# Attention beside a gated MLP on one core: query norm rows summed in one bank, key offset from a weight, gate by pairs

## Chip, core and metric

The kernel runs on one core of one Trainium2 chip. The metric is the device time in microseconds of one execution. The engines are called by their names in the profile: PE (TensorE), ACT (ScalarE), DVE (VectorE), POOL (GpSimd) and SP (the queue that issues most DMAs).

## What is computed

x is 2048 tokens by 448 features. Cut to what matters:

```python
xn = layernorm(x)
q, k, v = split(xn @ wqkv)            # 16 heads of 28
s = softmax(q @ k.T * 28**-0.5) @ v   # per head, 2048 x 2048 scores
s = s @ wo
g = silu(gelu_tanh(xn @ w1 + b1) @ w2 + b2)   # 448 -> 1792 -> 448
out = x + s * g
```

All inputs and the output are bfloat16.

## The kernel before

**Tiles.** The heads form four groups (g) of four, the queries four chunks (c) of 512. A block is a pair (g, c), 16 in all, run in the order b = 4g + c. Inside a block there are 16 key tiles of 128 for each of four heads: 64 units of 128 keys x 512 queries, 1024 units in the kernel (the last block is cut along the queries so that its end can be finished in pieces). A unit is a score matmul into a PSUM bank (`t_score`, L1158), an exp that turns it into a bfloat16 tile P, and a PV matmul (`pv_task`, L1417) that adds to the accumulator bank `acc`. Head features are padded from 28 to 32, so four heads fill the 128 partitions: score matmuls are row tiles, PV matmuls column tiles of the PE array.

**Two places for exp.** Most units get their exp on ACT (`p_exps`, L1217), which reads two or three banks of the PSUM ring in one instruction. The others, called late units, are done on DVE (`p_late`, `p_exp2`): the score goes into a side bank (ring bank 3 or the bank `misc`), L1262 moves it scaled to SBUF, and three scalar_tensor_tensor instructions (L1347, L1348, L1350) on one or two units at a time turn it into a bfloat16 exp by a polynomial. The result lies in one of five plates until PV has used it.

**Offset of the exp.** Each query and key carries a 29th feature. On the key side it is -1, on the query side a norm term: half the sum of squares of the query plus a constant from the norms of the key weights (`colK`). Thus a score has an upper bound taken off, and no maximum over keys is needed. The key's -1 is added at eviction (`t_kev`, L727, with the column `ecol[:, 2:3]`). The query's term is made tile by tile in `p_q`: eviction (L946), square (L951), a matmul with the selector `bsel` that sums the squares of each head into row 28 of its 32 (L953, in a second bank), and L956, which adds that bank, the constant and the query. The first chunk of group 0 has a path of its own (`p_q0`).

**The other branch.** The first layer (`p_f1`, L1011) is projected between attention blocks and kept in SBUF. At unit GM = 582 ACT switches its table and does all gelus in one stage (`p_gelu`, L1066), half from SBUF and half from PSUM (`p_direct`, which takes the ring; bank 3 is then not free for others). The second layer (`p_f2`, L1087 with eviction L1092) follows as soon as a chunk's gelu is done, so its first tile runs inside the gelu stage; then tanh on ACT and the gate on DVE tile by tile (`p_silu`, L1102 and L1105), and at the end `p_out`/`p_last`.

**What sets the order.** Each engine's instructions are written in a fixed order that is found while the program is built. Every piece of work is a generator that yields tasks with an engine, estimated durations, the buffers read and written, and a priority; `run` repeatedly takes the task that could start first, and among those within 0.1 us the best priority. Free PSUM banks go to the generators in the order of their numbers (`settle`). How many units become late is decided by `pick(k)`: DVE's backlog must not exceed `THS` of the block (in us), and the work must fit into what is left of the block plus `SLACKS` of the block:

```python
left = (n - 1 - r) * 0.452 + SLACKS[m // 64]
...
return (k == 1 or bl <= THS[m // 64]) and bl + k * (LC + 0.69) <= left
```

**Buffers of P.** `NP` buffers of 512 columns take the results of ACT's exps. From the time when the staged weights are no longer needed until 24 units before the gelu stage, free parts of the buffer h serve as 21 more, and after it parts of xnT as 15 more (`p_room`). An exp waits until the PV of its buffer's former unit has run.

**Queues.** Loads and stores go over SP in program order, and a DMA that waits there for an engine holds those behind it. The load of w2 is such a one; it is issued when the later scratch of DVE (in kT) has replaced the one inside w2's buffer.

Of the kernel before, what the change touches and what calls it, by code (L numbers as in the profile page):

```python
# [8 lines left out]
ALU = mybir.AluOpType  # L9
# [15 lines left out]
NRING = 6  # L25
NP = 21
NBLK = G * C
# [3 lines left out]
LC = 1.85  # L31
THS = (1.0, 6.0, 6.0, 6.0, 6.0, 5.0, 5.0, 5.0, 6.0, 6.0, 6.0, 6.0, 9.0, 6.0, 6.0, 6.0)
SLACKS = (9.0, 9.0, 9.0, 9.0, 8.5, 9.0, 7.0, 6.5, 6.5, 9.0, 9.5, 9.0, 8.5, 9.0, 9.0, 9.0)
SM_SCALE = DH ** -0.5
# [39 lines left out]
class _Kernel:  # L74
# [21 lines left out]
    def sb(self, name, shape, dtype=dt.bfloat16):  # L96
        return self.es.enter_context(self.nc.sbuf_tensor(name, shape, dtype))
# [160 lines left out]
    def alloc(self):  # L258
# [17 lines left out]
        self.E_sb = sb("E_sb", [128, 2, 512], bf)  # L276
        self.qsq = sb("qsq", [128, 2, 512], bf)
        self.ident = sb("ident", [128, 128], bf)
        self.bsel = sb("bsel", [128, 128], bf)
        self.sel = sb("sel", [128, 4], bf)  # L280
        self.iota_p = sb("iota_p", [128, 1], f32)
        self.ecol = sb("ecol", [128, 4], f32)
# [70 lines left out]
        self.b_wz, self.b_h2s = B(), B()  # L353
        self.b_qsq = [B(), B()]
        self.b_rc, self.b_rhl, self.b_colK, self.b_csq = B(), B(), B(), B()
# [19 lines left out]
        self.s_x2 = [self.sem("s_x2%d" % q) for q in range(4)]  # L375
        self.s_b1 = self.sem("s_b1")
        self.s_x0b, self.s_wqk1 = self.sem("s_x0b"), self.sem("s_wqk1")
        self.s_out = [self.sem("s_out%d" % q) for q in range(10)]
        self.s_w = {n: self.sem("s_" + n) for n in ("wqk", "wv", "w1", "w2", "wo", "b")}

    def schedule(self):
# [9 lines left out]
        K.stg_done = 0  # L391
        K.qsqs = [0, 1]
        K.f2n = [0] * C
        K.pv_started = False
# [58 lines left out]
        for c in (1, 2, 3):  # L453
            K.spawn(K.p_q(1, c), nxt())
        f1 = deque(SBT)
        for c in range(C):
            for _ in range(4):
                K.spawn(K.p_f1(*f1.popleft()), nxt())
            K.spawn(K.p_k(2, c), nxt())
            K.spawn(K.p_q(2, c), nxt())  # L460
        while f1:
            K.spawn(K.p_f1(*f1.popleft()), nxt())
        for c in range(C):
            K.spawn(K.p_k(3, c), nxt())
            K.spawn(K.p_q(3, c), nxt())
        K.spawn(K.p_gelu(), 0)
        K.spawn(K.p_direct(), 0)
# [14 lines left out]
    def constants(self):  # L482
# [3 lines left out]
        def f(eng):  # L486
# [12 lines left out]
            return eng.memset(K.xn[:, :, :, D:D + 1], 1.0)  # L499
        e(DVE, f, writes=[K.b_pads], dur=1.6)  # L500

        def late_pads():
# [49 lines left out]
        def f(eng):  # L552
# [3 lines left out]
        e(POOL, lambda eng: eng.tensor_copy(selb, K.sel[:, :, None].to_broadcast([128, 4, 32])), reads=[K.b_bsel],  # L556
          writes=[K.b_selb], dur=0.3)
        K.b_hf[1][0].r.append(K.b_bsel.w)

# [161 lines left out]
    def t_kev(self, E, g, c, bank, tok, prio=2):  # L721
        K = self
        dst = K.kT[:, g, c * 512:(c + 1) * 512]
        if E == ACT:
            fn = lambda eng: eng.activation(dst, bank, ACTF.Identity, bias=K.ecol[:, 2:3])
        else:
            fn = lambda eng: eng.tensor_scalar(dst, bank, K.ecol[:, 2:3], None, op0=ALU.add)  # L727
        return _Task(E, fn, [tok, K.b_cols], [K.b_kT[g][c]], 0.75, 0.0, prio)

# [20 lines left out]
    def p_first(self):  # L750
# [66 lines left out]
        def kproj(h):  # L817
            bank, tok = ring(4 * h + 1)
            for k in range(2):
                yield proj(1, h, k, bank, tok)  # L820
            yield _Task(ACT, lambda eng: eng.activation(K.kT[:, 0, 256 * h:256 * h + 256], bank[:, 0:256], ACTF.Identity,
                                                        bias=K.ecol[:, 2:3]),
                        [tok, K.b_cols] + ([K.b_kT0] if h else []), [K.b_kT[0][0] if h else K.b_kT0], 0.45, 0.0, 1 + h)
# [65 lines left out]
    def p_norm(self, g0, g1, pr=1):  # L889
        K = self  # L890
        bank, tok = yield ("bank",)
        n = g1 - g0

        def f(eng):
            ins = None
            for g in range(g0, g1):
                for kt in range(KT):
                    ins = eng.matmul(bank[:, g:g + 1], K.wsq[:, kt, 128 * g:128 * (g + 1)], K.ones[:, :],
                                     start=(kt == 0), stop=(kt == KT - 1), skip_group_check=True)
            return ins  # L900
        yield _Task(PE, f, K.b_wsq[g0:g1] + [K.b_pads], [tok], 0.15 * n + 0.1, 0.1, pr, 0.15)
        for b in K.b_hf[1]:
            b.r += [x.w for x in K.b_wsq[g0:g1]] + K.b_wsq[g0].r
        yield _Task(DVE, lambda eng: eng.tensor_copy(K.csq[:, g0:g1], bank[:, g0:g1]), [tok], [K.b_csq], 0.17, 0.0, pr)

        def f(eng):
            return eng.matmul(bank[:, 8 + g0:8 + g1], K.bsel[:, :], K.csq[:, g0:g1], start=True, stop=True)
        yield _Task(PE, f, [K.b_csq, K.b_bsel], [tok], 0.05, 0.15, pr)
        yield _Task(DVE, lambda eng: eng.tensor_scalar(K.colK[:, g0:g1], bank[:, 8 + g0:8 + g1], KNORM, K.coff[:, 0:1],
                                                       op0=ALU.mult, op1=ALU.add), [tok, K.b_cols], [K.b_colK], 0.17, 0.0, pr)  # L910
        K.banks.append((bank, tok))
# [27 lines left out]
    def p_q(self, g, c):  # L939
        K = self  # L940
        bank, tok = yield ("bank", lambda: K.ready(K.b_xnT[c] + [K.b_wqk[0][g], K.b_colK, K.b_kT[0][3]]) and ((g, c) == (0, 1) or K.boot()))
        for k in range(2):
# [4 lines left out]
        K.banks.append((bank, tok))  # L947
        yield ("until", lambda: len(K.qsqs) > 0)
        i = K.qsqs.pop(0)
        qs, tq = K.qsq[:, i, :], K.b_qsq[i]  # L950
        yield _Task(DVE, lambda eng: eng.tensor_tensor(qs, qb, qb, ALU.mult), [qr], [tq], 0.43, 0.0, 2)  # L951
        bank2, tok2 = yield ("bank", lambda: K.ready([tq]) and (g == 0 or K.norms_done))
        yield _Task(PE, lambda eng: eng.matmul(bank2, K.bsel[:, :], qs, start=True, stop=True),  # L953
# [3 lines left out]
                                                              op1=ALU.add), [tok2, K.b_colK, qr], [qr, K.b_qT[g][c]], 0.75, 0.0, 2)  # L957
        K.banks.append((bank2, tok2))

    def t_v(self, ts, h0, h1, bank, tok):  # L960
# [117 lines left out]
    def p_f2(self, c, t):  # L1078
        K = self
        bank, tok = yield ("bank", lambda: K.b_h[c].tw is not None and K.ready([K.b_h[c], K.b_w2]) and (c < 2 or K.g_done[c - 2]))  # L1080
        hv = K.h[:, c, :].rearrange("p (f n) -> p f n", n=512)
# [15 lines left out]
    def p_silu(self, c):  # L1097
# [5 lines left out]
                    [K.b_fsb[c % 2]], [K.b_sig[c % 2]], 0.1 + 0.375 * nt, 0.0, 0)  # L1103
        for t in range(nt):
            yield _Task(DVE, lambda eng, t=t: eng.scalar_tensor_tensor(K.g_sb[:, c, t, :], sg[:, t, :], 1.0, fb[:, t, :],  # L1105
                                                                       op0=ALU.add, op1=ALU.mult),
                        [K.b_sig[c % 2], K.b_fsb[c % 2]], [K.b_h[c], K.b_g[c]], 0.63, 0.0, 3)
        K.g_done[c] = True
# [498 lines left out]
```

The softmax here doesn't subtract the row's maximum and nothing guards it: scores larger than these inputs give would overflow.

## Time and profile before

The time is 472.9 us (median of three runs, 472.8 to 472.96); the profiled execution spans 471.2 us.

| engine | busy, us | share of span |
|---|---|---|
| ACT | 459.1 | 97% |
| PE | 439.9 | 93% |
| DVE | 408.6 | 87% |
| POOL | 42.5 | 9% |

| group (line, engine) | count | mean ns of one |
|---|---|---|
| L1217 ACT exp of two units | 202 | 1108 (into P) |
| L1217 ACT exp of three units | 171 | 1551 (into P) |
| L1066 ACT gelu, gelu stage from 256 to 283 us | 14 | up to 2345 |
| L1347, L1348, L1350 DVE exp by polynomial, two units | 153 | 1223 (L1347) |
| L951 DVE square of the query | 15 | 423 |
| L1105 DVE gate | 15 | 620 |
| L878 PE matmuls on a zero weight that keep PE busy | 684 | 220 |

The means of instructions that overlap their neighbours include the overlap, so count times mean is more than the busy time. PE's share contains L878, work that changes no result (a zero weight), and so is no measure of how full PE is. A line in the costliest groups gives busy time, mean duration of one, and the idle time of the engine just before, with what ended it.

### The profile page before, as it was taken

To read this page: it belongs to the slowest core of one execution; us is meant where nothing else is said; L and a number is where in the kernel's file an instruction comes from. 1 tells how busy PE (TensorE), PEld (TensorE's weight loads), DVE (VectorE), ACT (ScalarE), POOL (GpSimd) and SP (SyncE) were. 2 spreads that over 40 slices of the span, in tenths; PEclk is the share of its full clock that TensorE was granted. 3 is DMA by queue.
4 is the path that set the end of the run, shared out by engine and by line. 5 is a ranking of instruction groups with operands and counts; after the bars stand their busy time and mean duration, and the time that the engine had idled before them with its cause. 6 is when DMAs were issued, how large, how long until landed. Compare 5 with 4: busy or idle time off the path is not lost.

```text
span 471.2 us, 10607 instructions
## 1 busy us (share of the span) xinstructions
PE 439.9 (93%) x4407; PEld 175.2 (37%) x4440; DVE 408.6 (87%) x581; ACT 459.1 (97%) x417; POOL 42.5 (9%) x78
## 2 busy tenths in 40 slices
PE   6999999999999999999999999999999989999995
PEld 5442333333323233323333343333333443433552
DVE  8946999899899998998898959768898988989986
ACT  6999999999999999999999999999999999999994
POOL 7480100001000101001010100010010000010001
PEclk9999999999999999999999999999999999999999
DMA  8401000000000000000220000000110010101001
GB/s 265 141 2 36 2 1 0 1 2 2 1 0 1 1 1 2 2 0 1 70 69 2 1 0 1 11 30 1 41 39 1 1 40 3 40 1 40 3 22 60
DMA packets 8289, 11.11 MB, mean 24 GB/s; under 512 B 1649, under 2 KB 6897, under 8 KB 8242
## 3 DMA queue, kind: packets, MB, share of 16 engines
q1 hardware_dynamic: 7954, 9.75, 6.7%
q8 instruction: 35, 0.57, 0.5%
q10 hardware_dynamic: 288, 0.69, 0.4%
q14 instruction: 12, 0.10, 0.1%
HBM read 8.61 MB, written 1.84 MB: 22 GB/s over the span
## 4 chain that ended last, share of the span: by engine, by line
PE 46%; ACT 39%; issue 13%; DVE 1%; ACTq 0%; DVEq 0%
ACT P L1217 23%; PE ring L1158 12%; ACT h L1217 9%; PE acc L1417 7%; ACT xnT L1217 6%; PE ring L1028 5%; PE acc L878 4%; PE ring L1087 4%; PE misc L1087 3%; PE misc L716 2%; PE ring L716 2%; PE ring L970 1%; PE misc L1028 1%; PE acc L860 1%; PE misc L970 1%
## 5 line engine op out<-in xcount | busy, mean ns | idle before, releaser
L1217 ACT ACTIVATE P<-ring 128x1024 bf16<-128x1024 f32 x210 | 237.8, 1305 | 0.6 <-PE ring L1158 0.6
L1158 PE MATMUL ring<-qT,kT 32*128 32x512 bf16 (+2 forms) x1086 | 144.8, 359 | 16.6 <-ACT P L1217 6.4
L1217 ACT ACTIVATE h<-ring 128x1536 bf16<-128x1536 f32 (+1 forms) x97 | 111.3, 1292 | 1.0 <-PE acc L1417 0.7
L1158 PEld LDWEIGHTS ring<-qT,kT 32*128 32x128 bf16 x1086 | 37.5, 91 | 139.0 <-ACT P L1217 68.9
L1217 ACT ACTIVATE xnT<-ring 128x1536 bf16<-128x1536 f32 x66 | 77.6, 1350 | 0.0
L878 PE MATMUL acc<-ident,zero 128*128 128x128 bf16 x684 | 55.5, 220 | 0.5 <-issue 0.5
L1262 DVE TENSOR_SCALAR x_sb<-misc 128x512 f32<-128x512 f32 x64 | 44.0, 688 | 8.8 <-PE misc L1158 7.8
L1417 PE MATMUL acc<-P,vaug 128*32 128x512 bf16 (+2 forms) x587 | 50.0, 357 | 0.3 <-DVE x_sb L1350 0.3
L1489 POOL CAST rhi<-rc 128x16 bf16<-128x16 f32 x15 | 12.4, 824 | 395.2 <-DVE rc L1487 291.8
L878 PEld LDWEIGHTS acc<-ident,zero 128*128 128x128 bf16 x684 | 39.2, 98 | 21.5 <-issue 19.1
L1262 DVE TENSOR_SCALAR x_sb<-ring 128x512 f32<-128x512 f32 x43 | 29.6, 688 | 12.6 <-PE ring L1158 12.5
L1347 DVE SCALAR_TENSOR_TENSOR kT<-x_sb 128x1024 f32<-128x1024 uint16 (+1 forms) x32 | 38.1, 1189 | 1.8
L1348 DVE SCALAR_TENSOR_TENSOR kT<-kT 128x1024 f32<-128x1024 f32 (+1 forms) x32 | 37.8, 1183 | 0.4
L1028 PE MATMUL ring<-xnT,w 128*128 128x512 bf16 x141 | 36.6, 381 | 0.9 <-issue 0.8
L1087 PE MATMUL ring<-w,h 128*128 128x448 bf16 x140 | 33.9, 355 | 0.0
L1347 DVE SCALAR_TENSOR_TENSOR w<-x_sb 128x1024 f32<-128x1024 uint16 (+1 forms) x24 | 27.6, 1149 | 0.1
L1348 DVE SCALAR_TENSOR_TENSOR w<-w 128x1024 f32<-128x1024 f32 (+1 forms) x24 | 27.6, 1150 | 0.1
L1158 PE MATMUL misc<-qT,kT 32*128 32x512 bf16 (+1 forms) x66 | 24.6, 377 | 0.2 <-DVE w L1092 0.2
L1417 PE MATMUL acc<-h,vaug 128*32 128x512 bf16 x239 | 24.0, 384 | 0.0
L1350 DVE SCALAR_TENSOR_TENSOR x_sb<-kT,x_sb 128x1024 uint16<-128x1024 f32 x19 | 23.2, 1219 | 0.2
L1028 PE MATMUL misc<-xnT,w 128*128 128x512 bf16 x68 | 19.2, 381 | 1.1 <-issue 0.8
L1087 PE MATMUL misc<-w,h 128*128 128x448 bf16 x84 | 20.0, 355 | 0.0
(179 smaller groups left out, 550.9 us busy)
## 6 DMA issues: line engine op xcount, KB each, us to landing
h<-in_A_x_dram SPq DMA_DIRECT2D x4, 448.0 KB, 3.3
w<-in_B_w_dram SPq DMA_DIRECT2D x1, 1568.0 KB, 7.4
w<-in_B_w_dram SPq DMA_DIRECT2D x1, 1344.0 KB, 8.1
out_dram<-h SPq DMA_DIRECT2D x6, 224.0 KB, 2.0
x_sb<-in_A_x_dram SPq DMA_DIRECT2D x2, 448.0 KB, 5.8
h<-in_A_wqkv_dram SPq DMA_DIRECT2D x3, 168.0 KB, 5.3
x_sb<-in_A_x_dram ACTq DMA_DIRECT2D x1, 448.0 KB, 5.1
out_dram<-h SPq DMA_DIRECT2D x4, 112.0 KB, 1.7
```

The source lines that it names most:

```text
L716: ins = eng.matmul(bank, w[:, kt, g * 128:(g + 1) * 128], K.xnT[:, kt, c * 512:(c + 1) * 512], start=(kt == 0), stop=(kt == KT - 1))
L878: ins = eng.matmul(K.acc[:, 0:128], K.zero[:, :], K.ident[:, :], start=False, stop=True, skip_group_check=True)
L1028: ins = eng.matmul(bank, K.w1[:, kt, ft * 128:(ft + 1) * 128], K.xnT[:, kt, c * 512:(c + 1) * 512], start=(kt == 0), stop=(kt == KT - 1))
L1087: ins = eng.matmul(ps, hv[:, ft, t * 128:(t + 1) * 128], K.w2[:, ft, :], start=(ft == 0), stop=(ft == FT - 1))
L1158: return eng.matmul(dst, K.kT[32 * j:32 * j + 32, g, t * 128:(t + 1) * 128], K.qT[32 * j:32 * j + 32, g, c * 512 + q0:c * 512 + q0 + nq], ...
L1217: return eng.activation(reg[:, i0:i0 + n, :], K.ring[:, b0:b0 + n, :], ACTF.Exp, scale=SM_SCALE)
L1262: yield _Task(DVE, lambda eng, i=i, half=half, bank=bank: eng.tensor_scalar(K.ysb[i][:, 512 * half:512 * half + 512], bank, SM_SCALE * LOG ...
L1347: yield _Task(DVE, lambda eng: eng.scalar_tensor_tensor(u, lo, EXP_A, lo, op0=ALU.add, op1=ALU.mult), ty, [tu], d, 0.0, 4)
L1348: yield _Task(DVE, lambda eng: eng.scalar_tensor_tensor(u, u, EXP_B, u, op0=ALU.add, op1=ALU.mult), [tu], [tu], d, 0.0, 4)
L1350: yield _Task(DVE, lambda eng: eng.scalar_tensor_tensor(pl.bitcast(dt.uint16), u, EXP_K, y, op0=ALU.mult, op1=ALU.add), ty + [tu], [K.b_pl ...
L1417: return eng.matmul(K.acc[32 * j:32 * j + 32, q0:q0 + nq], K.vaug[:, t, 4 * g + j, :], ap[:, col:col + nq], tile_position=(0, 32 * j), sta ...
L1489: yield _Task(POOL, lambda eng: eng.tensor_copy(K.rhi[:, :], K.rc[:, :]), [K.b_rc], [K.b_rhl], 1.1, 0.0, 1)
```

## The change

It has five parts, and new values of the planner's thresholds.

- Query norm, groups 1 to 3: a tile is only evicted and squared. When all four chunks of a group are squared (four buffers `qsq`), four column-tiled matmuls with a narrow selector `bsel4` put the sums of all of them into one bank, one chunk per 32 partitions. One tensor_scalar adds the constants (`colK2`) and writes `qst`, and four DMAs on SP copy four rows each into the rows 28, 60, 92 and 124 of qT. Group 0 keeps the old path.
- Key offset: a -1 is written once into the weight wk, at the row that meets the feature of xn that is always 1. Key evictions are then plain copies.
- Gate: two tiles in one instruction.
- Side bank in gelu: `p_f2` doesn't start before all gelus from PSUM have been placed, so that `misc` serves late units until then.
- The new buffers take the room of three P buffers: NP goes from 21 to 18.

```diff
-NP = 21
+NP = 18
...
-THS = (1.0, 6.0, 6.0, 6.0, 6.0, 5.0, 5.0, 5.0, 6.0, 6.0, 6.0, 6.0, 9.0, 6.0, 6.0, 6.0)
-SLACKS = (9.0, 9.0, 9.0, 9.0, 8.5, 9.0, 7.0, 6.5, 6.5, 9.0, 9.5, 9.0, 8.5, 9.0, 9.0, 9.0)
+THS = (1.0, 5.0, 11.0, 6.0, 6.0, 5.0, 6.0, 5.0, 6.0, 6.0, 6.0, 6.0, 6.0, 6.0, 5.0, 11.0)
+SLACKS = (6.0, 7.0, 8.0, 10.0, 8.0, 6.0, 7.5, 8.5, 9.0, 7.5, 5.5, 8.0, 10.0, 10.0, 7.5, 4.5)
...
-        self.qsq = sb("qsq", [128, 2, 512], bf)
+        self.qsq = sb("qsq", [128, 4, 512], bf)
+        self.qst = sb("qst", [128, 512], bf)
...
+        e(DVE, lambda eng: eng.memset(K.wk[64:65, 3, :].rearrange("p (h e) -> p h e", e=32)[:, :, DH:DH + 1], -1.0),
+          writes=[K.b_pads], dur=0.1)
...
+        bs4 = K.bsel[:, :].rearrange("p (j e) -> p e j", e=32)[:, 24:32, :]
+        e(POOL, lambda eng: eng.tensor_copy(K.bsel4[:, :].rearrange("p (e j) -> p e j", j=4), bs4), reads=[K.b_bsel],
+          writes=[K.b_bsel4], dur=0.2)
...
-            fn = lambda eng: eng.tensor_scalar(dst, bank, K.ecol[:, 2:3], None, op0=ALU.add)
+            fn = lambda eng: eng.tensor_copy(dst, bank)
...
+    def p_qn(self, g):
+        K = self
+        bank, tok = yield ("bank", lambda: len(K.qn[g]) == C and K.ready(K.b_qsq) and K.norms_done)
+
+        def f(eng):
+            ins = None
+            for c in range(C):
+                ins = eng.matmul(bank[32 * c:32 * c + 32, :], K.bsel4[:, :], K.qsq[:, c, :], tile_position=(0, 32 * c),
+                                 start=True, stop=True, skip_group_check=True)
+            return ins
+        yield _Task(PE, f, K.b_qsq + [K.b_bsel4], [tok], 0.226, 0.17, 4, mode="col")
+        K.qn_done = g
+        yield _Task(DVE, lambda eng: eng.tensor_scalar(K.qst[:, :], bank, K.colK2[:, g:g + 1], None, op0=ALU.add),
+                    [tok, K.b_colK2], [K.b_qst], 0.75, 0.0, 2)
+        K.banks.append((bank, tok))
+        for c in range(C):
+            dst = bass.AP(tensor=K.qT, offset=28 * G * S + g * S + 512 * c, ap=[[32 * G * S, 4], [1, 512]])
+            K.dma(SP, lambda eng, c=c, dst=dst: eng.dma_start(dst, K.qst[32 * c + 16:32 * c + 20, :]), K.s_qn[g][c],
+                  reads=[K.b_qst, K.qn[g][c]], writes=[K.b_qT[g][c]], land=max(K.now, K.b_qst.tw) + 2.5)
...
-        bank, tok = yield ("bank", lambda: K.b_h[c].tw is not None and K.ready([K.b_h[c], K.b_w2]) and (c < 2 or K.g_done[c - 2]))
+        bank, tok = yield ("bank", lambda: K.b_h[c].tw is not None and K.ready([K.b_h[c], K.b_w2]) and K.dir_read == len(DIRECT) and (c < 2 or K.g_done[c - 2]))
...
-        for t in range(nt):
-            yield _Task(DVE, lambda eng, t=t: eng.scalar_tensor_tensor(K.g_sb[:, c, t, :], sg[:, t, :], 1.0, fb[:, t, :],
-                                                                       op0=ALU.add, op1=ALU.mult),
-                        [K.b_sig[c % 2], K.b_fsb[c % 2]], [K.b_h[c], K.b_g[c]], 0.63, 0.0, 3)
+        for t0 in range(0, nt, 2):
+            t1 = min(t0 + 2, nt)
+            yield _Task(DVE, lambda eng, t0=t0, t1=t1: eng.scalar_tensor_tensor(
+                K.g_sb[:, c, t0:t1, :], sg[:, t0:t1, :], 1.0, fb[:, t0:t1, :], op0=ALU.add, op1=ALU.mult),
+                        [K.b_sig[c % 2], K.b_fsb[c % 2]], [K.b_h[c], K.b_g[c]], 0.15 + 0.467 * (t1 - t0), 0.0, 3)
```

## The prediction

> **What bounds the kernel now.** I read the page's busy shares first, then its slices, then the chain that ended last, then the waits of ScalarE and of VectorE, and last the timeline around the gelu stage. Busy shares and slices:
>
> ```profile
> PE 439.9 (93%) x4407; PEld 175.2 (37%) x4440; DVE 408.6 (87%) x581; ACT 459.1 (97%) x417; POOL 42.5 (9%) x78
> ...
> DVE  8946999899899998998898959768898988989986
> ACT  6999999999999999999999999999999999999994
> ```
>
> ScalarE (ACT) is at 97%, and its only loose slices are the first and the last. In the windows from 40 to 250 us it is busy 208.95 of 210 us, from 312 to 465 us 152.99 of 153. The chain of waits says "ACT P L1217 22.7%" first, yet also names PE often; so I looked at ScalarE's own waits. The largest after the first exp (12.46 us) are these:
>
> ```profile
> ACT h L1217 <- PE acc L1417: 0.7, 1, 0.7
> ...
> ACT P L1217 <- PE ring L1158: 0.6, 2, 0.3
> ```
>
> Between first and last exp ScalarE waits 1.6 us at most (these two groups and one wait of 0.3). Nothing is won by making other engines faster for their own sake. The time falls only if ScalarE gets fewer instructions, or starts or ends earlier. The one way to give it fewer is the share of score tiles whose exp VectorE (DVE) computes ("late" units in the code). Their count and price are in the costliest groups:
>
> ```profile
> L1262 DVE TENSOR_SCALAR x_sb<-misc 128x512 f32<-128x512 f32 x64 | 44.0, 688 | 8.8 <-PE misc L1158 7.8
> L1262 DVE TENSOR_SCALAR x_sb<-ring 128x512 f32<-128x512 f32 x43 | 29.6, 688 | 12.6 <-PE ring L1158 12.5
> ```
>
> So 64 + 43 = 107 of 1024 units go to VectorE. A late unit costs 0.688 us here plus half of three double-width instructions (L1347, L1348, L1350: 1223, 1215 and 1219 ns), 1.83 us: 2.52 us of VectorE. On ScalarE I take the timeline from 309.31 to 318.34 us: eight exps, alternately of three and two units, 20 units in 9.03 us, 0.4515 us each. The exchange rate of this kernel: 2.52 us freed on VectorE takes 0.45 us off the end, if it is filled with a late unit.
>
> **What the Trainium skill says.** "Perfetto Trace Analysis", section "Identifying the Most-Contended Engine", says to judge ScalarE and VectorE by occupancy and to improve the fullest engine first; the trace agrees on ScalarE (97%, 1.6 us of waits). "VectorE: DVE Perf Modes", section "The TRN2 errata", gives (N+151)/0.96 ns for a two-tensor fp32 operation at one element a cycle: 624 ns at 448 elements, where this trace's gate (L1105) has 620, so the form holds here. "TensorE: Matmul & The Clock Gate", Part 3, says that column tiles run side by side, one matmul long plus some 4 ns each. The trace agrees: a round of eight column-tiled PV matmuls (L1417) takes 0.61 us, two matmuls' time. "DMA: Bandwidth & Descriptors", section "Anatomy of one DMA", gives about 2 us fixed for a small transfer; here 112 KB stores land in 1.7 us.
>
> **The change part by part.**
>
> Query norm. For groups 1 to 3, twelve instructions at L956 go. Their rows:
>
> ```profile
> L956 DVE SCALAR_TENSOR_TENSOR qT<-ring,colK,qT 128x512 bf16<-128x512 f32 x9 | 6.7, 748 | 2.0 <-PE ring L1158 1.2 <-PE ring L953 0.5
> L727 DVE TENSOR_SCALAR kT<-ring,ecol 128x512 bf16<-128x512 f32 x9 | 6.7, 746 | 3.1 <-PE ring L716 3.1
> L946 DVE CAST qT<-misc 128x512 bf16<-128x512 f32 x9 | 6.2, 688 | 1.1 <-PE misc L716 1.0
> ```
>
> The fifteen take 6.7 + 4.4 = 11.1 us, 0.74 each, twelve 8.9 us. Three new tensor_scalars of the same shape and source as L727 cost 3 x 0.746 = 2.2. Net 6.7 us freed on VectorE. The squares (L951) stay. On PE twelve matmuls become three packed groups, some 2 us less, off the path. The norm also held a side bank (ring 3 or misc) in the twelve cases for some 1.1 us (matmul 0.38, eviction 0.74); nine such holds vanish, 10 us of bank time. VectorE waits 20.3 us in total for late scores (7.8 + 12.5 above), partly for lack of a bank; I count half a unit for this.
>
> The placement DMA adds a wait: the first score of blocks 4, 8 and 12 needs four norm rows written by the SP queue. What is queued behind it on PE are all later scores, and ScalarE waits for those. In the trace of before the last L956 of groups 1, 2 and 3 starts at 100.33, 173.69 and 249.27 us. The copies of the finished sums at L1477, at 132.24, 233.41 and 364.87, mark the ends of blocks 3, 7 and 11; even with scores 10 us ahead of those there are over 20, 50 and 100 us. A DMA of 2 us, 4 us if it queued behind others, is hidden: 0.
>
> Key's -1 from a weight. Fifteen L727 become copies like L946: 15 x (0.747 - 0.688) = 0.9 us freed. The two early ones on ScalarE stay the same size. The added memset of sixteen elements lies on VectorE ahead of the first bn_stats. Its neighbours of this size take 0.06 us, and one dependency more on its own engine shows 0.14 (end of L499 to the next start); the first x tile lands at about the same time (3.6 us). Between 0 and 0.2 us at the start; I take 0.1. The added GpSimd copy (its neighbour L556: 0.29 us) delays the square of wk at 7.08 to 8.01, but the matmuls that read it start at 9.48: 0.
>
> Gate by pairs. Fifteen L1105 become eight (two pairs for three chunks, a pair and a single for the last). A pair by the formula above is (896+151)/0.96 = 1.09 us against 1.24: 7 x 0.15 = 1.1 us freed.
>
> Side bank in gelu. The timeline of VectorE there:
>
> ```profile
> 270.98 0.69 DVE L1262 TENSOR_SCALAR x_sb<-misc 128x512 f32<-128x512 f32 x1 [0.30 <-PE misc L1158]
> ...
> 279.78 0.62 DVE L1092 TENSOR_TENSOR w<-misc,b2b 128x448 bf16<-128x448 f32 x1 [3.14 <-PE misc L1087]
> 280.89 0.69 DVE L1262 TENSOR_SCALAR x_sb<-misc 128x512 f32<-128x512 f32 x1 [0.48 <-PE misc L1158]
> 282.66 0.69 DVE L1262 TENSOR_SCALAR x_sb<-misc 128x512 f32<-128x512 f32 x1 [1.08 <-PE misc L1158]
> ```
>
> The first tile of the second layer holds misc from 271.7 to 280.4, and VectorE idles 3.14 + 0.48 + 1.08 = 4.7 us. With misc kept for late units that is 4.7/2.52 = 1.9, say 2 units (0 to 3: the five result plates can run out). The tile itself goes after 280. The second layer ends with its last eviction at 369.38 and feeds the output of block 12, whose sums end at 387.91: 6 us later is hidden.
>
> NP 21 to 18. In the first 35 us only these buffers serve the exps. Nine pairs now fit where ten did. The PV rounds that free eight each end at 21.56, 24.49, 28.45 and 31.06; pair 10 would start at 21.6, pair 14 at 25.2, pair 18 at 28.8, pair 22 at 32.5. The first is a near touch, the others have 0.4 us or more. I take 0.1 us, with up to 3 as the bad end.
>
> Thresholds THS and SLACKS. They move late units between blocks. The trace can't price them. SLACKS falls for nine of the blocks 1 to 15 and rises for six; I take 0, with -4 to +5 units.
>
> Sum: (6.7 + 0.9)/2.52 = 3.0 units, gate 0.4, gelu 2, bank 0.5: 5.9 units, 113 late in place of 107. VectorE is busy 190.83 of 210 us in the stretch where most is freed, so I convert 90% there: 5.6. Times 0.4515: -2.5 us. Start +0.2. From 472.9: 470.6, and I state 470.5.
>
> **Rivals.** (1) Freed time isn't filled. VectorE already idles 62 us of 471, mostly waiting for a bank or a score, so capacity may not be what limits the late units. Then only the gelu part, or nothing, comes: 472.0 to 473.2, at 472.7. For it: the 20.3 us of waits for late scores. Against: outside gelu VectorE is nine tenths busy in nearly every slice. (2) More than the sum: freed banks and moved thresholds let VectorE use some of its idle time too, ten units or more, 468.3. For it: 10.6 us idle from 270 to 310. Against: idle pieces there are 1 to 3 us between dependent steps. (3) Slower. Eighteen exp buffers make ScalarE wait for PV in the first 35 us (four rounds at up to 0.8 us, one projection's time, 3 us), or the thresholds lose four units (1.8 us) and late units at a block's end hold up its PV. With no gain that is 474.7 to 476, at 475. For it: PE is at 9.7 of 10 there, so PV can slip. Against: ScalarE's waits there are only 0.3 us now, and two of the four rounds have spare time.
>
> **Numbers.** Forecast 0.54, (1) 0.18, (2) 0.13, (3) 0.15. Faster than 471.95: the forecast nearly whole, (2), and a fifth of (1), 0.70; within 0.2%: most of (1) and a little of the forecast, 0.15; slower 0.15. The range 468.3 to 473.7 leaves out half of (2)'s best cases and most of (3).
>
> **What would show it.** Right: the L1262 groups add to 112 to 114, some two more of them between 271 and 281 us; ScalarE still without waits after the first exp; the first exp within 0.2 us of 12.46; the four-row DMAs landing over 10 us before the scores that need them. Wrong: ScalarE waits on PE before 35 us or at the start of a block; the late count at 107 or below with VectorE less busy; a wait of PE for the SP queue's writes.

## The result and the profile after

The kernel after takes 470.71 us (470.54 to 471.0 in six runs), the kernel before 472.9: a ratio of 0.9954, 95% interval 0.9942 to 0.9967. The forecast was 470.5, range 468.3 to 473.7. The profiled spans are 471.2 and 468.6 us. All later ratios are to the kernel before on the same chip in the same session; differences to it are taken to its median there (472.95 to 473.26 us), and differences to the kernel after from the times as given, which leaves some 0.3 us of doubt.

The page of the kernel after, busy shares and two of the slices (one digit per fortieth of the span, tenths busy):

```profile
PE 435.8 (93%) x4322; PEld 169.3 (36%) x4352; DVE 412.0 (88%) x580; ACT 456.4 (97%) x415; POOL 47.0 (10%) x79
...
DVE  8947998898999899999898998999799998999975
ACT  6999999999999999999999999999999999999994
```

ScalarE still sets the time: 97%, loose only in the first and last slice. Its waits after the first exp (line of the waiting instruction, what it waited for; us in total, times, longest):

```profile
ACT P L1267 <- PE ring L1208: 0.8, 2, 0.5
...
ACT h L1267 <- PE ring L1208: 0.4, 1, 0.4
ACT xnT L1267 <- PE ring L1208: 0.3, 1, 0.3
```

They add to 1.5 us, as against 1.6 before. So in sum the waits did not change; ScalarE has less to do. The costliest groups say how much less (L1312 answers to L1262 of before):

```profile
L1312 DVE TENSOR_SCALAR x_sb<-misc 128x512 f32<-128x512 f32 x57 | 39.2, 688 | 8.3 <-PE misc L1208 7.7
L1312 DVE TENSOR_SCALAR x_sb<-ring 128x512 f32<-128x512 f32 x55 | 37.8, 688 | 8.3 <-PE ring L1208 8.2
```

57 + 55 = 112 late units in place of 107. From the first exp to the end of the last exp it is 449.38 us in place of 452.16, of which ScalarE works 448.28 in place of 450.71. That is 2.43 us of work for five units, 0.49 each (forecast 0.4515): one exp of two units and one of three are gone (202 and 171 before, 201 and 170 after). The first exp starts at 12.54 us (12.46 before), and from the end of the last exp to the end of the span, called the tail from here on, it is 6.7 us (6.6 before). Together: -2.78 + 0.08 + 0.1 = -2.6, the difference of the spans.

**Where the five units are.** The windows of the late evictions alone, first of the kernel before, then of after (window in us, its length, VectorE's busy time on that line with the count, granted clock, DMA share, GB/s; an eviction that crosses an edge counts on both sides):

```profile
40.00:250.00 210.00, 35.04 (x51) 1.00 0.04 10
250.00:312.00 62.00, 11.03 (x16) 1.00 0.03 9
312.00:465.00 153.00, 27.55 (x40) 1.00 0.06 20
```

```profile
40.00:250.00 210.00, 36.30 (x53) 1.00 0.04 10
250.00:312.00 62.00, 14.08 (x22) 1.00 0.03 9
312.00:465.00 153.00, 26.63 (x39) 1.00 0.07 22
```

Counted by start they are 51 / 16 / 40 before and 53 / 21 / 38 after. The stretch with the freed norm and key work gained two units, the stretch around the gelus five (two of them before 285 us, 12 for 10, and three after it, 9 for 6), and the rest lost two. In the gelu stage VectorE's timeline answers to the one shown of before:

```profile
270.33 1.22 DVE L1400 SCALAR_TENSOR_TENSOR x_sb<-kT,x_sb 128x1024 uint16<-128x1024 f32 x1
271.65 0.69 DVE L1312 TENSOR_SCALAR x_sb<-misc 128x512 f32<-128x512 f32 x1
...
273.59 0.69 DVE L1312 TENSOR_SCALAR x_sb<-misc 128x512 f32<-128x512 f32 x1
...
276.78 0.69 DVE L1312 TENSOR_SCALAR x_sb<-misc 128x512 f32<-128x512 f32 x1
...
278.86 0.69 DVE L1312 TENSOR_SCALAR x_sb<-misc 128x512 f32<-128x512 f32 x1 [0.26 <-PE misc L1208]
...
283.55 0.62 DVE L1141 TENSOR_TENSOR w<-misc,b2b 128x448 bf16<-128x448 f32 x1 [0.35 <-PE misc L1136]
```

The 4.7 us of idle time between 271.7 and 282.7 us are gone. From 267 to 283 us six late evictions start where the kernel before has four, a gain of two, and the second layer's first eviction (L1141) has moved from 279.78 to 283.55 us.

The edited instructions themselves (gate by pairs, key evictions, norm rows) cost what was forecast (1.09, 0.688 and 0.746 us):

```profile
L1155 DVE SCALAR_TENSOR_TENSOR h<-w 128x896 bf16<-128x896 bf16 x7 | 7.6, 1084 | 0.2 <-ACT w L1151 0.2
...
L743 DVE CAST kT<-ring 128x512 bf16<-128x512 f32 x8 | 5.5, 689 | 2.8 <-PE ring L732 2.7
...
L1001 DVE TENSOR_SCALAR qst<-ring,colK 128x512 bf16<-128x512 f32 x2 | 1.5, 746 | 0.2 <-PE ring L996 0.2
```

The placement of the norm rows, seen from the tile `qst` (duration minimum / median / maximum in ns, first and last start in us):

```profile
L1006 SPq DMA_DIRECT2D qT<-qst x12: 497/497/592, 97.8 to 231.9; - x12
L1001 DVE TENSOR_SCALAR qst<-ring,colK x2: 742/746/751, 97.1 to 159.4; 128x512 bf16<-128x512 f32 x2
```

The third `qst` follows at 229.5 us. The rows leave at 97.8 us and later for scores of a block that begins around 127 us (the sums of block 3 are copied at 126.77), and at the latest at 231.9 us for one around 362. The profile gives no landing time for them, but there are over 20 us from issue to use, and no wait of PE on these DMAs appears: they are hidden.

### The profile page after: what moved, and what is told of

Same layout as the page of the kernel before. It is cut to its first block, busy times and chain, and to the rows that moved or that the text cites. A ratio compares the mean times of both kernels' runs of the same rounds, so it can differ in the third digit from the quotient of the medians.

```text
span 468.6 us, 10353 instructions
## 1 busy us (share of the span) xinstructions
PE 435.8 (93%) x4322; PEld 169.3 (36%) x4352; DVE 412.0 (88%) x580; ACT 456.4 (97%) x415; POOL 47.0 (10%) x79
## 4 chain that ended last, share of the span: by engine, by line
ACT 48%; PE 32%; issue 14%; DVE 4%; DMA 1%; ACTq 0%; DVEq 0%
ACT P L1267 25%; ACT h L1267 12%; PE ring L1208 9%; ACT xnT L1267 8%; PE ring L1077 5%; PE acc L1467 5%; PE acc L893 3%; PE misc L1077 2%; PE misc L1136 1%; PE misc L732 1%; PE ring L1136 1%; PE ring L1566 1%; ACT w L1151 1%; PE ring L732 1%; DVE x_sb L1312 1%
## 5 line engine op out<-in xcount | busy, mean ns | idle before, releaser
L1267 ACT ACTIVATE P<-ring 128x1024 bf16<-128x1024 f32 (+1 forms) x196 | 224.4, 1296 | 0.8 <-PE ring L1208 0.8
L1267 ACT ACTIVATE h<-ring 128x1024 bf16<-128x1024 f32 (+1 forms) x103 | 121.2, 1298 | 0.4 <-PE ring L1208 0.4
L1267 ACT ACTIVATE xnT<-ring 128x1536 bf16<-128x1536 f32 (+1 forms) x72 | 84.4, 1334 | 0.3 <-PE ring L1208 0.3
L893 PE MATMUL acc<-ident,zero 128*128 128x128 bf16 x594 | 49.4, 220 | 0.0
L1312 DVE TENSOR_SCALAR x_sb<-misc 128x512 f32<-128x512 f32 x57 | 39.2, 688 | 8.3 <-PE misc L1208 7.7
L1312 DVE TENSOR_SCALAR x_sb<-ring 128x512 f32<-128x512 f32 x55 | 37.8, 688 | 8.3 <-PE ring L1208 8.2
L893 PEld LDWEIGHTS acc<-ident,zero 128*128 128x128 bf16 x594 | 33.6, 98 | 21.2 <-issue 20.2
L1136 PE MATMUL misc<-w,h 128*128 128x448 bf16 x154 | 36.1, 355 | 0.1
L1400 DVE SCALAR_TENSOR_TENSOR x_sb<-kT,x_sb 128x1024 uint16<-128x1024 f32 (+1 forms) x21 | 24.6, 1171 | 0.4
L1467 PE MATMUL acc<-xnT,vaug 128*32 128x512 bf16 (+2 forms) x240 | 19.3, 329 | 0.4 <-ACT P L1267 0.4
L1077 PEld LDWEIGHTS ring<-xnT,w 128*128 128x128 bf16 x156 | 12.4, 98 | 17.9 <-issue 6.1
```

The costliest lines, as they stand in the source:

```text
L893: ins = eng.matmul(K.acc[:, 0:128], K.zero[:, :], K.ident[:, :], start=False, stop=True, skip_group_check=True)
L1077: ins = eng.matmul(bank, K.w1[:, kt, ft * 128:(ft + 1) * 128], K.xnT[:, kt, c * 512:(c + 1) * 512], start=(kt == 0), stop=(kt == KT - 1))
L1136: ins = eng.matmul(ps, hv[:, ft, t * 128:(t + 1) * 128], K.w2[:, ft, :], start=(ft == 0), stop=(ft == FT - 1))
L1267: return eng.activation(reg[:, i0:i0 + n, :], K.ring[:, b0:b0 + n, :], ACTF.Exp, scale=SM_SCALE)
L1312: yield _Task(DVE, lambda eng, i=i, half=half, bank=bank: eng.tensor_scalar(K.ysb[i][:, 512 * half:512 * half + 512], bank, SM_SCALE * LOG ...
L1400: yield _Task(DVE, lambda eng: eng.scalar_tensor_tensor(pl.bitcast(dt.uint16), u, EXP_K, y, op0=ALU.mult, op1=ALU.add), ty + [tu], [K.b_pl ...
```

## The experiments

One table first. "Norm" is the new query norm with the key weight, "bank" the side bank kept in gelu, "thr" the new THS and SLACKS, P the number of P buffers; late units are counted by the start of their eviction before 250 us, from 250 to 312, and after.

| kernel | norm | bank | gate pairs | thr | P | time, us | ratio | late units |
|---|---|---|---|---|---|---|---|---|
| before | - | - | - | - | 21 | 472.9 | | 51+16+40 = 107 |
| e1 | - | - | - | - | 18 | 476.5 | 1.0069 | 51+17+38 = 106 |
| e8 | - | yes | yes | - | 21 | 474.47 | 1.0024 | 51+19+37 = 107 |
| e12 | - | yes | yes | yes | 21 | 473.03 | 1.0001 | 51+20+35 = 106 |
| e2 | yes | - | - | - | 18 | 472.13 | 0.9977 | 53+18+40 = 111 |
| e3 | yes | - | yes | yes | 18 | 472.77 | 0.9995 | 53+16+38 = 107 |
| e4 | yes | yes | yes | - | 18 | 475.21 | 1.0038 | 53+19+38 = 110 |
| after | yes | yes | yes | yes | 18 | 470.71 | 0.9954 | 53+21+38 = 112 |
| e5 | yes | yes | yes | yes | 21 | 471.0 | 0.9949 | 53+21+38 = 112 |

**Buffers: the kernel before with 18 (e1).**

```diff
-NP = 21
+NP = 18
```

> The kernel before with 18 exp buffers in place of 21 and nothing else. Theory (time follows the count of late units at 0.45 us each, and the loss of buffers is nearly free, as the prediction had it, 0.1 us): the built order has 106 late units, one fewer than before, so 472.9 + 0.45 + 0.1 = 473.4. Rival (the buffers are a real cost that other parts of the change have to pay back): ScalarE waits for PV of the former unit, at block ends above all; 475 to 477, with new waits of ScalarE on PE summing to 2 us or more.

Measured: 476.5 us, ratio 1.0069 (1.0052 to 1.0086), 3.4 us slower. ScalarE's waits:

```profile
ACT h L1217 <- PE acc L1417: 1.6, 1, 1.6
ACT P L1217 <- PE ring L1158: 1.0, 4, 0.3
...
ACT xnT L1217 <- PE ring L1158: 0.5, 1, 0.5
```

With one more of 0.4 they add to 3.5 us (1.6 before). None of what was added lies in the first 35 us, where the prediction had looked: the 1.6 us wait for PV is at 109.97 us, at the end of a block, where the kernel before waits 0.7, and the other new ones are at block ends too. ScalarE's idle time between first and last exp rises from 1.45 to 3.58 us, it works 0.96 us more for the one late unit lost (which it does as an exp of one unit alone), and the tail grows by 0.16: together the 3.25 us between the profiled spans. The price of 0.1 us was wrong for this order.

**Buffers: the kernel after with 21 (e5).** The new buffers are laid into the room of w2, which is loaded later.

```diff
-NP = 18
+NP = 21
...
-        self.qsq = sb("qsq", [128, 4, 512], bf)
-        self.qst = sb("qst", [128, 512], bf)
+        self.qsq = w2f[:, 0:2048].rearrange("p (b n) -> p b n", n=512)
+        self.qst = w2f[:, 4096:4608]
...
-            yield ("until", lambda: K.late_blk >= 2 * C)
+            yield ("until", lambda: K.late_blk >= 2 * C and K.qn_sent == 3)
```

> The changed kernel with 21 exp buffers again; qsq and qst lie in parts of the buffer w2 that are unused until w2 is loaded, and the load waits for their last readers. All thresholds as changed; the built order has the same 112 late units. Theory A (e1 showed a property of that one order, not of 18 buffers: where the thresholds leave no wait for PV, three buffers are worth nothing): 470.7, at most 0.3 less. Theory B (18 buffers cost some 3 us in every order, as in e1, and the changed kernel carries that cost): 468 or less.

Measured: 471.0 us, ratio 0.9949 (0.9937 to 0.9962), with the same 112 late units and waits of 1.5 us. Giving the three buffers back brings nothing. So the 3.4 us of the run before are no price of three buffers as such; they are what the order of the kernel before, with its thresholds, loses when it is replanned with 18.

**Norm and key weight alone (e2)**, on the kernel before: no gate by pairs, no side bank in gelu, old thresholds, 18 buffers (edit against the kernel after, thresholds aside).

```diff
-        bank, tok = yield ("bank", lambda: ... and K.dir_read == len(DIRECT) and (c < 2 or K.g_done[c - 2]))
+        bank, tok = yield ("bank", lambda: ... and (c < 2 or K.g_done[c - 2]))
...
-        for t0 in range(0, nt, 2):
+        for t in range(nt):
```

> The new query norm and the key's -1 from the weight, with 18 buffers; gate, side bank in gelu and thresholds as before. The built order has 111 late units, 4 more than before. Theory: 472.9 - 4 x 0.45 + 0.2 at the start = 471.3, nearly the whole gain. Rival (the gain belongs to the side bank in gelu and the thresholds, the norm only moves work): within 0.5 us of 472.9.

Measured: 472.13 us, 0.9977 (0.9966 to 0.9988), 1.0 us better, with 111 late units: less than the theory's 1.6, more than the rival's 0.5. Two of the four more lie before 250 us. ScalarE works 1.9 us less than in the kernel before, but the tail is 0.97 us longer (7.55) and the first exp 0.13 later; those take over half of it back.

**Side bank taken away (e3)** from the kernel after (the first of the two edits above alone).

> The changed kernel with the second layer again free to start inside the gelu stage, so that it takes the side bank; all else, thresholds too, as changed. The built order has 107 late units in place of 112, two of the five lost in the gelu stage's block. Theory: 470.7 + 5 x 0.45 = 473.0. Rival (the late units of the gelu stage are off the path, since ScalarE does gelus then and they only move): within 0.5 us of 470.7.

Measured: 472.77 us, 0.9995 (0.9987 to 1.0004), 107 late units: five fewer than after, and 2.1 us. VectorE's timeline shows the old hole:

```profile
274.22 1.22 DVE L1400 SCALAR_TENSOR_TENSOR x_sb<-kT,x_sb 128x1024 uint16<-128x1024 f32 x1
279.72 0.62 DVE L1141 TENSOR_TENSOR w<-misc,b2b 128x448 bf16<-128x448 f32 x1 [4.28 <-PE misc L1136]
280.82 0.69 DVE L1312 TENSOR_SCALAR x_sb<-misc 128x512 f32<-128x512 f32 x1 [0.48 <-PE misc L1208]
```

4.28 + 0.48 us idle while the second layer's first tile holds misc. That two of the five units go into this hole is seen: from 250 to 285 us there are 10 here and 12 in the kernel after, and every kernel that keeps the bank has 12 to 14 there, every one that doesn't 10 or 11. The other three start from 285 to 312 us (6 here, 9 after). They do not follow from the later start of the second layer as such: e4, e8 and e12 have that too, and only 7, 7 and 8 units there. Why just this order fits nine in stays open.

**Side bank and gate pairs alone (e8)**, on the kernel before with its thresholds.

> The kernel before with the side bank kept for VectorE in gelu and the gate by pairs, thresholds of before, 21 buffers. The prediction's sum gives these two parts 2.4 late units, 1.1 us, 471.8. But the built order has 107 late units, two more in the gelu block and two fewer elsewhere. Theory (count decides): 472.9 within 0.7. Rival (the gelu stage is worth its own gain, whatever happens elsewhere): 471.8.

Measured: 474.47 us, 1.0024 (1.0016 to 1.0032): slower by 1.2 us, and the late units are 107 as before, 51+19+37. Three more from 250 to 312 us (two of them before 285), three fewer after it, and the tail is 0.70 us longer. So the bank is worth its two units in the hole here too, and they are lost again later. That isn't the old thresholds' doing alone: with the new ones (e12) five are missing there.

**Old thresholds in the kernel after (e4).**

```diff
-THS = (1.0, 5.0, 11.0, 6.0, 6.0, 5.0, 6.0, 5.0, 6.0, 6.0, 6.0, 6.0, 6.0, 6.0, 5.0, 11.0)
-SLACKS = (6.0, 7.0, 8.0, 10.0, 8.0, 6.0, 7.5, 8.5, 9.0, 7.5, 5.5, 8.0, 10.0, 10.0, 7.5, 4.5)
+THS = (1.0, 6.0, 6.0, 6.0, 6.0, 5.0, 5.0, 5.0, 6.0, 6.0, 6.0, 6.0, 9.0, 6.0, 6.0, 6.0)
+SLACKS = (9.0, 9.0, 9.0, 9.0, 8.5, 9.0, 7.0, 6.5, 6.5, 9.0, 9.5, 9.0, 8.5, 9.0, 9.0, 9.0)
```

> The changed kernel with the THS and SLACKS of before. The built order has 110 late units in place of 112. Theory: 470.7 + 2 x 0.45 = 471.6, and DVE may end later by up to 2 us, since the last block takes one late unit more: 471.6 to 473.5. Rival (thresholds are worth nothing, as the prediction took them): 470.7 within 0.3.

Measured: 475.21 us, 1.0038 (1.0023 to 1.0053): 4.5 us worse than after, and slower than before. That is above the theory's range too. Two late units (110) explain 1 us. The profiled spans differ by 4.8: ScalarE works 1.47 us more between first and last exp and is idle 0.35 more, the first exp is 0.52 us later (a wait of 0.8 us for the load of wqkv), and the tail is 9.2 us in place of 6.7. VectorE's timeline at the end:

```profile
456.47 1.22 DVE L1400 SCALAR_TENSOR_TENSOR plx<-kT,x_sb 128x1024 uint16<-128x1024 f32 x1
...
465.26 0.29 DVE L1501 CAST E_sb<-acc 128x128 bf16<-128x128 f32 x1
...
466.09 0.94 DVE L1515 RECIPROCAL w<-ring 128x128 f32<-128x128 f32 x1
...
470.88 0.39 DVE L1577 TENSOR_TENSOR h<-h 128x448 bf16<-128x448 bf16 x1
```

The last late units end at 457.69 us (L1400), 6.6 us before the last exp does; and after the last exp the pieces of the output are finished in a bunch, to 471.27 us. In the kernel after the last late unit ends 14.8 us before the last exp, the pieces are spread out, and the last L1577 starts at 466.10 us.

**The last block's threshold alone (e6)**: the kernel of the run before, with the new values for block 15 (THS 11.0, SLACKS 4.5).

> As e4 (changed kernel, thresholds of before), but THS and SLACKS of the last block as changed, 11 and 4.5 in place of 6 and 9. The built order has 109 late units, one fewer than e4, in the last block. Theory (e4 lost its time after ScalarE's last exp: a late unit of the last block ended too late): the stretch from the last exp to the end falls from 9.1 us to 6.6 to 7, and the time from 475.2 to 473.2 to 473.7. Rival (the loss lies in the middle, by other thresholds): 475 or more.

Measured: 473.4 us, 1.0005 (0.9996 to 1.0013), tail 6.9 us, first exp 12.55, 109 late units; the last late one ends 14.2 us before the last exp. The tail comes back (2.2 us), as the theory had it. The start comes back too (0.5 us), but not by the threshold: ScalarE's order is the same in both kernels up to 452 us, and what differs is the wait for the load of wqkv. One late unit less takes 0.7 us of it, and 1.8 us of the 4.5 remain won. What is left to the kernel after, 2.7 us, is three late units (1.4) and 0.2 us of tail. ScalarE works 2.2 us more between its first and last exp, 0.7 more than three units account for; it needs 373 exps for 371, one of them of a single unit (0.6 us). How much of the rest that makes stays open.

**Exchange rate (e7)**: the kernel after with at most 12 late units in block 9, where the gelu stage is.

```diff
-        if not 0 < sub < NBLK or r < 4:
+        if not 0 < sub < NBLK or r < 4 or len([x for x in K.late if x // 64 == sub]) >= (12 if sub == 9 else 99):
```

> The changed kernel, where the block of the gelu stage may take 12 late units and no more (17 before the cap); nothing else. The built order has 104 late units in place of 112, five fewer in that block and three elsewhere. VectorE gets lighter by 8 x 2.5 = 20 us. Theory (time follows the late count, 0.4515 us each): 470.7 + 8 x 0.45 = 474.3. Rival (late units are not what sets the time; a lighter VectorE answers sooner): 471 or less.

Measured: 474.31 us, 1.0022 (1.0015 to 1.0029), 104 late units. Eight fewer cost 3.6 us against the kernel after, 0.45 each, the forecast's price; against e5, the same 112 units measured in this run's own session, it is 3.3 us, 0.41 each. ScalarE works 452.15 us in place of 448.28, 0.48 a unit. The rival is out: with VectorE 18 us lighter the time rose. Here the time follows the count.

**Norm and key weight taken away (e12)** at the new thresholds: the kernel before with side bank, gate pairs and the new THS and SLACKS, so with 21 buffers.

> The kernel after with the old query norm and the old key eviction (so 21 buffers): gate by pairs, side bank in gelu and new thresholds stay. The built order has 106 late units where the kernel after has 112. Theory (the new norm and the key weight are worth the late units that their VectorE time carries, at 0.45 to 0.49 us of ScalarE each, here six units): 470.7 + 6 x 0.45 to 0.49 = 473.4 to 473.6 us. Rival (they are worth the 3 to 3.5 units of the prediction's sum, the rest of the gain is the thresholds'): 470.7 + 3.5 x 0.45 = 472.3 us or less.

Measured: 473.03 us, 1.0001 (0.9992 to 1.001), 106 late units. The upper end of the rival, 472.3, lies outside the interval; my figure, 473.4, is 0.4 us too high, so a unit was worth 0.39 here (0.52 by ScalarE's work, 451.39 us for 448.28). The windows of the late evictions (columns as above):

```profile
40.00:250.00 210.00, 35.07 (x51) 1.00 0.04 10
250.00:312.00 62.00, 13.75 (x20) 1.00 0.02 5
312.00:465.00 153.00, 24.08 (x35) 1.00 0.07 22
```

Of the six units only two are missing where the norm's work lies (51 for 53). Three are missing after 312 us, where the kernel after does no norm work at all. So these six units are not what the norm is worth; the larger part is lost where only the planned order differs. That new thresholds and old norm do not suit each other isn't shown by this: with the old thresholds (e8) the same kernel has one late unit more, but takes 1.1 to 1.4 us longer.

**More work for GpSimd (e9).** With 23 buffers, the squares of groups 1 to 3, the gate, and the addition of x for three of the four chunks go to GpSimd; thresholds and GM (594) were fitted to that.

```diff
-        yield _Task(DVE, lambda eng: eng.tensor_tensor(qs, qb, qb, ALU.mult), [qr], [tq], 0.43, 0.0, 2)
+        yield _Task(POOL if g else DVE, lambda eng: eng.tensor_tensor(qs, qb, qb, ALU.mult), [qr], [tq], 1.15 if g else 0.43, 0.05 if g else 0.0, 2)
...
+            yield _Task(POOL, lambda eng, t=t: eng.tensor_tensor(sg[:, t, :], sg[:, t, :], fb[:, t, :], ALU.mult),
+                        [K.b_fsb[c % 2]], [K.b_sig[c % 2]], 1.05, 0.05, 3)
+            yield _Task(POOL, lambda eng, t=t: eng.tensor_tensor(K.g_sb[:, c, t, :], sg[:, t, :], fb[:, t, :], ALU.add),
+                        [K.b_sig[c % 2], K.b_fsb[c % 2]], [K.b_h[c], K.b_g[c]], 1.05, 0.05, 3)
...
```

> The changed kernel with 23 exp buffers (qsq and qst inside w2, as in e5) and more of VectorE's work on GpSimd: the squares of groups 1 to 3, the additions of x for the first three chunks, and the gate of all but the last tile as a multiply and an add per tile. Thresholds, the start of the gelu stage (unit 594) and the planner's tie window (0.2 us) chosen for it. The built order has 114 late units. Theory (late count, plus ScalarE's waits and the stretch after its last exp): two units more than the changed kernel give 1.0 us, the rest is what the order saves in waits, up to 1 us: 468.7 to 469.7. Rival (GpSimd and VectorE get in each other's way in SBUF, and VectorE's instructions grow longer): VectorE's rows above 1.25 us for two units, 471 or more.

Measured: 473.92 us, 1.0023 (1.0015 to 1.0031), with 114 late units, two more than after. Here the count alone does not tell the time. ScalarE's waits, and then two of VectorE's groups by form (a polynomial step and the late evictions):

```profile
ACT P L1271 <- PE ring L1212: 2.1, 5, 0.5
ACT xnT L1271 <- PE ring L1212: 1.0, 4, 0.4
```

```profile
L1401 DVE SCALAR_TENSOR_TENSOR kT<-x_sb 128x1024 f32<-128x1024 uint16 x34 | 45.3, 1333 | 1.8
...
L1316 DVE TENSOR_SCALAR x_sb<-misc 128x512 f32<-128x512 f32 x57 | 39.1, 685 | 10.2 <-PE misc L1212 9.7
```

With two smaller ones the waits are 4.0 us, against 1.5, and the first exp comes 0.6 us later. The polynomial step takes 1333 ns; in the kernel after its row is this:

```profile
L1397 DVE SCALAR_TENSOR_TENSOR kT<-x_sb 128x1024 f32<-128x1024 uint16 x32 | 39.1, 1222 | 1.3
```

So VectorE's instructions come later than the fixed order had assumed, and that PE's scores come late through them is inferred. GpSimd's own are late too: the order was planned with 1.05 us for each multiply and add of the gate, and they took 1.44 and 1.66 us in the mean. The two were not separated. The timeline of GpSimd and of VectorE at one such place:

```profile
363.15 1.03 POOL L1158 TENSOR_TENSOR w<-w 128x448 bf16<-128x448 bf16 x1 [10.15 <-PE misc L1140]
```

```profile
363.49 1.77 DVE L1402 SCALAR_TENSOR_TENSOR kT<-kT 128x1024 f32<-128x1024 f32 x1
```

VectorE's step, 1.21 us where nothing interferes, begins while GpSimd's multiply runs to 364.18 us, and ends at 365.26: 1.08 us after it, nearly a whole step. "SBUF — State Buffer" of the Trainium skill, section "Who interferes with whom", says that a VectorE instruction with two SBUF inputs contends with a GpSimd instruction that reads SBUF, and that the later one blocks until the other is done. This trace agrees, and also in what is spared: the evictions from PSUM (L1316) keep their 685 ns.

**Squares and additions on GpSimd, the gate back on VectorE (e10)** (thresholds fitted again, GM 586).

> As e9 without the gate on GpSimd: only squares and additions of x move. Gelu stage from unit 586, tie window 0.15 us. 114 late units. Theory: as e9, 469 to 470. Rival as for e9.

Measured: 470.99 us, 0.9955 (0.994 to 0.9969), 114 late units. GpSimd's square of 128x512 takes 1676 ns, the polynomial step 1275. With two more late units than after I would have put it 0.9 us lower, and 469 to 470 was expected. The traces say where that went: ScalarE works 0.69 us less than in the kernel after, but is idle 0.60 us more between first and last exp, starts its first exp 0.17 later, and the tail is 0.20 longer.

**Thresholds fitted again, 23 buffers, all on VectorE (e11)** (GM 581).

> The changed kernel with 23 exp buffers, nothing moved to GpSimd, wider THS and SLACKS and a tie window of 0.15 us. 111 late units, one fewer than the changed kernel. Theory of the count alone: 470.7 + 0.5 = 471.2, less up to 0.7 for waits of ScalarE that go away. Rival (room in buffers and thresholds lets the same VectorE work end sooner): 470 or less.

Measured: 470.38 us, 0.9944 (0.9929 to 0.9959), 111 late units, waits of 1.0 us, between theory and rival. Here the count is off by its own measure: with one unit more to do than in the kernel after, ScalarE works no longer (448.21 us for 448.28). Why was not settled; it shows that the price of a single unit is not sharp. This and the two kernels next to it (e5, e10) cannot be told from the kernel after. No version was found that is clearly better than it.

## Why the prediction held, and where its steps failed

The time was right within 0.2 us, and the mechanism was the right one: ScalarE stays the bound, VectorE takes over more exps, at some 0.45 us each. The late units were forecast at 113 and are 112; the run with a cap (e7) puts the rate at 0.41 to 0.45. Rivals (1) and (3) did not come about, though single parts of the change did end there. The sum was right with several wrong terms, so that the hit within 0.2 us is in part luck.

- **Freed work.** The sizes per instruction held to 0.01 us. VectorE's busy time rose by 3.4 us while five units brought 5 x 2.52 = 12.6, so 9.2 us were freed (8.7 forecast).
- **Conversion of the freed time before the gelus** (3.0 units and 0.5 for the banks, at 90%). This failed: two units came, not three. Every kernel with the new norm has 52 to 54 late units before 250 us, every one without it 51. VectorE is busy 190.83 us there before and 188.35 after: 7.6 us freed less two units (5.0) leave 2.5 us idle. The rate is two thirds, from a view that showed VectorE nine tenths busy; but units come whole, and one unit more would have made it one.
- **Gelu** (2 units, and 0.4 for the gate). Right for the hole of 4.7 us: it filled with the two units that the timeline gave, in every order with the bank. What became of the gate's 0.4 can't be read from whole units.
- **From 285 to 312 us** (none). Three units came, in idle time that only rival (2) counted (5.3 us before from 285 to 310, 2.0 after). They are of this order: with the old thresholds (e4) one comes, and without the bank (e3) none.
- **After 312 us** (none). Two units were lost. That this and the three units above nearly offset each other is luck.
- **Start** (+0.1 us). The first exp came 0.08 us later; but among all kernels run, with and without the memset, it lies between 12.33 and 13.14 us, so this hit says nothing on the memset.
- **P buffers** (0.1 us). The view was wrong: only the first 35 us were looked at. In the order of before, three buffers fewer cost 3.4 us, of which 2.1 are idle time of ScalarE at the ends of later blocks; in the order of after, nothing.
- **Thresholds** (0, with -4 to +5 units). The size was wrong: in the kernel after the new values are worth 4.5 us by the times (4.0 by the ratios, and 0.5 of the 4.5 may be the late load), of which two units are 1 us; the last block's value takes the tail from 9.2 to 6.9 us. The prediction counted thresholds in late units only and had no term for the tail.
- **Placement DMA** (0). Right as far as the trace shows: nothing waits on it.

Counted one way, the split is quite another than forecast: with the thresholds of before, the edits make the kernel 2.1 us slower (e4; 2.4 faster were forecast), and the new thresholds then bring 4.5 us (0 were forecast). Counted other ways it is different again, for the parts do not add up. From the kernel after, taking the thresholds away costs 4.5 us, the norm 2.3, the bank 2.1: together 8.9 us (8.1 by the ratios), of a whole gain of 2.2. From the kernel before, norm and key weight with 18 buffers bring 1.0 us, bank and gate lose 1.2, the three together without the thresholds lose 2.1. Each edit makes the program plan another order, and orders with the same work differ by one to three late units and up to 2.4 us of tail.

What the new thresholds are worth depends on the rest: 4.0 to 4.5 us in the kernel after, 1.1 to 1.4 without the new norm (e8 to e12), and with the norm but without the bank they lose 0.6 to 0.9 (e2 to e3, gate pairs included).

What can be given to a part on its own is what repeats in all orders: two units before the gelus for the norm and key weight (before to e2, e8 to e4, e12 to the kernel after), and two from 250 to 285 us for the side bank (before to e8 and e2 to e4, both with the gate, and e3 to the kernel after, the bank alone). From 285 to 312 us the same three pairs give one more, one fewer and three more.

## What to carry over

Where engines follow an order planned ahead, forecast the bound engine's work from time freed elsewhere, and be careful with the rate: here some two thirds were filled, where nine tenths of the stretch were busy, and work that comes in whole units leaves a rest. Don't read the worth of a part from taking it out of a tuned kernel, since the losses of the parts can add to several times the whole gain; look instead for the count in the stage where the part acts, across several kernels. And look at the tail after the bound engine's last instruction as a term of its own: late units that ended 6.6 us before the last exp went with a tail 2.4 us longer, as much as five units are worth elsewhere. It is not the only cause of a long tail: in e2 they end 11.7 us before it, and the tail is still 0.8 us longer than after.

## What was not expected of the hardware

GpSimd's multiplications and additions of 128x448 bfloat16, 1.03 and 1.09 us in the kernel after, took 1435, 1655 and 1781 ns in the mean in the run with the gate on GpSimd (e9). The means hide two kinds: of the 42 instructions 14 took 1.03 to 1.04 us and 28 took 1.75 to 2.12, nothing between. VectorE's polynomial step went from 1222 to 1333 ns. Moving work off a full VectorE to a GpSimd busy for a tenth of the span thus went with two more late units and 2.5 us of added ScalarE waits.
